# An adaLN block with a long S4D convolution and a ReLU FFN: the last twelve of sixteen kernel values from three powers instead of two more doublings, and wider DVE steps in the shift of h and the butterflies

## The chip, the cores and the metric

The kernel runs on one core of one Trainium2 chip. The metric is the device time of one execution in microseconds, the median over the runs shown. Start times in the trace count from the start of the profiled span.

## The reference

One sequence of 2048 tokens with 576 channels passes through an S4D convolution and then through a ReLU FFN, each behind a layer norm that is shifted and scaled by six vectors made from a condition `c`. What matters of it:

```python
dt = jnp.exp(log_dt)
A = -jnp.exp(log_A_real) + 1j * A_imag          # 576 channels x 128 states
C = (C_real + 1j * C_imag) * dt[:, None]
P = jnp.exp((A * dt[:, None])[:, :, None] * pos[None, None, :])   # pos = 0..2047
K = 2.0 * jnp.einsum("dn,dnl->dl", C, P).real   # the long kernel
y = irfft(rfft(u, 2 * L) * rfft(K, 2 * L))[:L]  # per channel
_A_ref = y + u * D_skip

mod = (_silu(c) @ w_mod).reshape(c.shape[0], 6, 1, -1)
sa, ca, ga, sb, cb, gb = (mod[:, i] for i in range(6))
h = _layernorm(x) * (1 + ca) + sa
x = x + ga * _A_ref(h, ...)
h = _layernorm(x) * (1 + cb) + sb
x = x + gb * (jnp.maximum(h @ w1, 0) @ w2)      # 576 -> 4608 -> 576
```

Everything is float32.

## The kernel before, in words

The tokens are taken in four blocks of 512. The convolution is done blockwise in the frequency domain: `conv(s)` transforms the kernel's block s and the tokens' block s by DFT matmuls on PE (`transform`, PSUM tile `ps_f`, L852), a radix-4 butterfly on DVE (`butterfly1` L864 to 868, `butterfly2` L870 to 881), multiplies spectra of all earlier blocks (`product`, L1032 to 1038), and goes back. The FFN (`ffn`, from L1268) takes 36 chunks of 128 hidden channels for each block, 144 steps in all: PE makes the hidden chunk `hps` (L1332), ACT writes its rounded half `hh` (L1337), DVE the remainder `hl` (L1338), and PE multiplies both by `w2` (L1358).

The program has three parts in time.

*Kernel generation* (`KGen.first`, L318 on). K is needed as a sum over the states of C z^l, where z = exp(A dt). Position l is split as 32 a + b, so a matmul over the 128 states of W1 (sixteen values a, with C in them) and W2 (32 values b) gives the block. This is done in NG = 6 groups of G = 96 channels, each in two half groups u of H = 48. For each group:

- `exps`: PE makes the exponents (tile `ph`), ACT takes Exp of them (tile `E`).
- `turns`: PE makes the phases, ACT rounds them to whole turns (tile `k`, L59), DVE subtracts (L62, `k<-ph,k`). This is done in three pieces; the last holds the powers of z listed in `POWERS`.
- `sines`: ACT takes sines and cosines; DVE and POOL multiply them by the moduli into W2, and `powers` makes Zp, the powers 32, 64, 128 and 256 of z, in PSUM, with the powers 512 and 1024 in `zs` in SBUF. `moduli` multiplies Zp by E on DVE.
- `doubling`: from W1's first value the values two, then four, eight and sixteen. A doubling of m values multiplies the m that are there by the power 32 m, complex: two DVE products (`t` by the real part, `T` by the imaginary part) and two adds. The first two doublings take the whole group; the third (m = 4) and the fourth (m = 8) each half group alone. The adds of the first three are on DVE, those of the fourth on POOL (L68).
- `save`: W1 goes to DRAM for the later blocks; `products`: PE multiplies W2 by W1 (tile `kps`, L71), u = 0 at the end of its own group, u = 1 (`late`) between the phases of the next.

In this part all instructions of PE, ACT, DVE and POOL, but for some copies and memsets on POOL, are kept in the program's order by the recording helpers: `act` L59, `v` L62, `stt` L65, `pool` L68, `matmul` L71. That order is written out by hand in the loop over g: the phases of group g + 1 stand between the doublings of group g.

*Passage to conv(0).* `early` makes h, the normed and shifted tokens of block 0, in stages that the loop calls. In the last group (g = 5) its last stage runs between the third and the fourth doubling: `skip` adds the kernel's skip term to the first kernel tile `kt` (L1263), then h is multiplied by `ca` (L641) and gets `sa` added (L642), one token tile of 576 columns at a time. conv(0) then transforms `kt` (24 outputs with those of h, 48 records on PE), runs the products of the last group, stores its rows to DRAM (`kd`), loads the second tile `kt` back, and goes on to its butterflies and products. The queue of SP carries `kd` and `kt`, that of POOL carries `Rd`.

*The FFN with what remains.* The other blocks' kernels are made by rotating W1 further (`rest`, L482 to 488, products L517), and conv(1) to conv(3) run beneath the FFN. Each is a generator that yields the estimated DVE time of each piece; `step()`, called in each FFN chunk, draws pieces from the generator up to a budget per chunk. The order within the FFN is then made by a scheduler from these pieces. The butterfly's yields are 1.5 for each half of `butterfly1`, then 1.5 and 1.8 in `butterfly2`; those of the products are 1.35 for each instruction.

Of the kernel before, what the change touches and what calls it, by code (L numbers as in the profile page):

```python
# [34 lines left out]
POWERS = (32, 64, 128, 256, 512, 1024)  # L35
# [14 lines left out]
class KGen:  # L50
# [131 lines left out]
    def exps(self, g):  # L182

        E = self.E[g] = []
        for s0, n in ((0, 8), (8, 8), (16, 8), (24, 8), (32, 6)):
            e = self.pt.tile([P, 2, 8 * H], F32, tag="E", bufs=8, name=f"E_{g}")
            e = self.chunk(e, s0, n)
            self.act(e, self.times(g, self.zz[1], s0, n), AF.Exp)
            E.append(e)
            yield  # L190

    def turns(self, g):

        F = self.F[g] = []
        for s0, n in ((0, 8), (17, 8), (32, 6)):
# [66 lines left out]
    def powers(self, g, e, f):  # L262

        Z = self.ps.tile([P, 2, 512], F32, tag="Z", name=f"Zp_{g}")[:, :, 0 : 4 * G]
# [4 lines left out]
        self.act(by_u(Z[:, 1]), f[:, :, 0:4], AF.Sin, scale=-TWO_PI)  # L269
        self.act(by_u(zs[:, :, 1]), f[:, :, 4:6], AF.Sin, scale=-TWO_PI)  # L270
        self.cos(by_u(Z[:, 0]), c[:, :, 0:4])
        self.cos(by_u(zs[:, :, 0]), c[:, :, 4:6])
        for r in (1, 0):
            self.pool(by_u(zs[:, :, r]), by_u(zs[:, :, r]), e[:, :, 4:6], op=ALU.mult)
        self.Z[g] = Z, zs

        def moduli():
            for r in (1, 0):
                self.v(by_u(Z[:, r]), by_u(Z[:, r]), e[:, :, 0:4], ALU.mult)
# [3 lines left out]
    def doubling(self, g, i, u):  # L283

        v, p = self.v, self.pool
        Z = self.Z[g][0]
        m, n = 1 << i, (u.stop - u.start) * H
        W1 = self.W1[g][:, :, u].rearrange("p r u c a -> p r (u c) a")
        X, out = W1[:, :, :, 0:m], W1[:, :, :, m : 2 * m]
        zr, zi = (  # L290
            Z[:, r, i, u.start * H : u.stop * H].unsqueeze(1).unsqueeze(3)
            .broadcast_to([P, 2, n, m])
            for r in range(2)
        )
        if m == 8:
            t = self.pc.tile([P, 16 * H], F32, tag="T0", bufs=2, name="T0")
            T = self.pc.tile([P, 16 * H], F32, tag="T1", bufs=2, name="T1")
        else:
            t = self.pc.tile([P, 8 * H], F32, tag="t", bufs=2, name="t")[:, : 2 * n * m]
            T = self.ps.tile([P, 512], F32, tag="T", name="T")[:, : 2 * n * m]  # L300
        t, T = (x.rearrange("p (r c a) -> p r c a", r=2, c=n) for x in (t, T))
        v(t, X, zr, ALU.mult)
        v(T, X, zi, ALU.mult)
        yield
        add = p if m == 8 else v
        add(out[:, 0], t[:, 0], T[:, 1], op=ALU.subtract)
        add(out[:, 1], t[:, 1], T[:, 0], op=ALU.add)
# [16 lines left out]
    def first(self, setup, mod):  # L324
# [70 lines left out]
        for g in range(NG):  # L395
            self.moduli()
            if g + 1 == NG:
                next(early)
            double = [
                self.doubling(g, i, u)  # L400
                for i, u in (
                    (0, slice(0, 2)), (1, slice(0, 2)), (2, slice(0, 1)), (2, slice(1, 2)),
                    (3, slice(0, 1)), (3, slice(1, 2)),
                )
            ]
# [22 lines left out]
            run(*double[4:])  # L428
# [143 lines left out]
class Body:  # L572
# [34 lines left out]
    def early(self, kg):  # L607
# [32 lines left out]
        for i in (0, 2, 1, 3):  # L640
            kept(nc.vector.tensor_tensor(h[:, i], h[:, i], self.m["ca"], op=ALU.mult))  # L641
            kept(nc.vector.tensor_tensor(h[:, i], h[:, i], self.m["sa"], op=ALU.add))  # L642
# [921 lines left out]
```

## Time and profile before

| | |
|---|---|
| median of three runs | 1333.97 us (1328.8 to 1339.76) |
| profiled execution | 1333.12 us |
| its span | 1331.4 us |
| PE busy | 1209.0 us (91%) |
| DVE busy | 895.4 us (67%) |
| ACT busy | 494.5 us (37%) |
| POOL busy | 162.8 us (12%) |
| mean granted clock of PE | 0.945 |

The busy share of a whole span is a mean over stages with different limits, so it does not say what a saved microsecond is worth. For that the span is cut into windows, and in each the busy time of the engines is compared with the window's length. Rows of a timeline give the start, the length, the engine, the line, the operation with the names of output and inputs, the shape, and after `x` how many neighbouring instructions the row joins; a bracket behind it says how long the engine was idle before it and what ended that. In the chain of waits each row is a piece of the path that ended last. `L62` and its neighbours are helpers, so a row there is told apart by its tiles: `T<-W,Zp` is a product of a doubling, `k<-ph,k` a subtraction of whole turns, `W<-T,T` on POOL the adds of the last doubling.

### The profile page before, as it was taken

The page shows a single profiled execution, that of the slowest core. Times are in us where ns is not written, and L with a number is a line of the kernel's source. Part 1 is how long each engine was busy: PE and PEld are TensorE (multiplying, and loading weights), DVE is VectorE, ACT ScalarE, POOL GpSimd, SP SyncE. Part 2 cuts the span into 40 slices and gives each one's busy share as a digit, 9 for nine tenths or more (in the row PEclk, how much of TensorE's full clock was granted, in tenths as well). Part 3 has the DMA queues.
Part 4 walks back from the last instruction along what each step waited for, and adds up shares of the span by engine and source line. Part 5 has one row for each costly group of instructions (what it writes and reads, how often), then busy time and mean ns, then how long its engine had stood idle before and what let it go on. Part 6 is the DMA issues. An engine that isn't in the chain of part 4 may idle for free.

```text
span 1331.4 us, 25993 instructions
## 1 busy us (share of the span) xinstructions
PE 1209.0 (91%) x10720; PEld 956.7 (72%) x10720; DVE 895.4 (67%) x1324; ACT 494.5 (37%) x863; POOL 162.8 (12%) x260
## 2 busy tenths in 40 slices
PE   4566676989989999999999999999999999999997
PEld 3344554667767687777777887887888888888885
DVE  5989988999986999689468993558995231111112
ACT  5678623222223422622243225433223453232321
POOL 0756502011000100100001000100000000000000
PEclk9557788999999999999999999999999999999999
DMA  8557982989878967799879985868996557666651
GB/s 272 214 221 296 304 307 84 350 296 331 307 253 304 337 224 277 247 402 342 281 276 338 357 321 156 288 203 305 346 363 198 175 181 223 198 198 202 192 168 54
DMA packets 122379, 345.85 MB, mean 260 GB/s; under 512 B 23916, under 2 KB 24212, under 8 KB 111508
## 3 DMA queue, kind: packets, MB, share of 16 engines
q1 hardware_dynamic: 105364, 226.96, 51.2%
q0 software_dynamic: 16384, 115.85, 23.1%
q8 instruction: 84, 1.38, 0.4%
q10 hardware_dynamic: 512, 1.38, 0.3%
q14 instruction: 35, 0.29, 0.1%
HBM read 262.73 MB, written 81.40 MB: 258 GB/s over the span
## 4 chain that ended last, share of the span: by engine, by line
PE 68%; DVE 17%; DMA 7%; issue 4%; ACT 2%; POOL 1%; SPq 0%; ACTq 0%; DVEq 0%; POOLq 0%
PE acc L1358 28%; PE hps L1332 27%; PE ps_f L852 5%; DMA L1d<-w 3%; PE kps L71 2%; PE ph L71 2%; DVE T L482 2%; DVE W1r L484 2%; PE ps_i L1059 2%; PE kps L517 1%; DVE w L1302 1%; DVE W1r L486 1%; DVE W1r L488 1%; DVE w L1314 1%; DVE T L62 1%
## 5 line engine op out<-in xcount | busy, mean ns | idle before, releaser
L1332 PE MATMUL hps<-xh,w 128*128 128x512 f32 x1152 | 395.2, 403 | 1.2 <-ACT xh L47 1.2
L1358 PE MATMUL acc<-w,hh 128*128 128x512 f32 x1152 | 366.4, 400 | 3.3 <-ACT hh L1337 3.2
L1338 DVE SCALAR_TENSOR_TENSOR hl<-hps,hh 128x512 fp32r<-128x512 f32 x144 | 99.0, 687 | 311.5 <-ACT hh L1337 310.8
L1332 PEld LDWEIGHTS hps<-xh,w 128*128 128x128 f32 x1152 | 217.8, 190 | 49.7 <-ACT xh L47 2.5
L1358 PEld LDWEIGHTS acc<-w,hh 128*128 128x128 f32 x1152 | 215.1, 188 | 50.6 <-ACT hh L1337 4.1
L1332 PE MATMUL hps<-xl,w 128*128 128x512 f32 x576 | 228.5, 397 | 0.7 <-DVE xl L47 0.5
L1358 PE MATMUL acc<-w,hl 128*128 128x512 f32 x576 | 223.1, 399 | 1.8 <-DVE hl L1338 1.8
L1337 ACT ACTIVATE hh<-hps 128x512 fp32r<-128x512 f32 x144 | 86.0, 597 | 327.7 <-PE hps L1332 320.5
L1307 ACT ACTIVATE w<-r 128x576 fp32r<-128x576 f32 x141 | 96.7, 686 | 216.5 <-PE acc L1358 216.1
L1332 PEld LDWEIGHTS hps<-xl,w 128*128 128x128 f32 x576 | 109.4, 190 | 24.7 <-DVE xl L47 1.7
L1358 PEld LDWEIGHTS acc<-w,hl 128*128 128x128 f32 x576 | 107.7, 189 | 26.1 <-DVE hl L1338 3.7
L1297 ACT ACTIVATE w<-r 128x640 fp32r<-128x640 f32 x140 | 102.6, 733 | 59.1 <-DMA L1d<-w 53.8
L1332 PE MATMUL hps<-xs,w 128*128 128x512 f32 x288 | 97.8, 409 | 0.0
L71 PE MATMUL kps<-W,W 128*32 128x16 f32 x2304 | 39.6, 210 | 47.3 <-POOL W L68 28.4
L1038 DVE TENSOR_TENSOR Y<-Y,T 128x1152 f32<-128x1152 f32 x60 | 79.3, 1349 | 0.0
L71 PEld LDWEIGHTS kps<-W,W 128*32 128x32 f32 x2304 | 34.8, 143 | 60.7 <-POOL W L68 31.0
L853 ACT ACTIVATE Z<-ps_f 128x288 f32<-128x288 f32 x120 | 49.0, 410 | 70.5 <-PE ps_f L852 68.5
L517 PEld LDWEIGHTS kps<-W1r,W2r 128*32 128x32 f32 x3456 | 45.2, 113 | 38.4 <-issue 19.7
L517 PE MATMUL kps<-W1r,W2r 128*32 128x48 f32 (+2 forms) x3456 | 52.5, 202 | 15.6 <-ACT ker L527 9.4
L1478 POOL DMA_DIRECT2D out_dram<-x x16 | 8.7, 545 | 466.9 <-DVE x L1470 464.5
L1332 PEld LDWEIGHTS hps<-xs,w 128*128 128x128 f32 x288 | 53.2, 188 | 11.1
L1358 PE MATMUL acc<-hh,w 128*128 128x512 f32 x144 | 57.5, 399 | 0.0
(235 smaller groups left out, 1574.5 us busy)
## 6 DMA issues: line engine op xcount, KB each, us to landing
r<-in_w_dram SPq DMA_DIRECT2D x144, 320.0 KB, 6.0
r<-in_w_dram SPq DMA_DIRECT2D x144, 288.0 KB, 3.9
w<-L1d SPq DMA_DIRECT2D x108, 320.0 KB, 4.1
w<-L2d SPq DMA_DIRECT2D x108, 288.0 KB, 2.8
W2r<-W2d POOLq DMA_DIRECT2D x18, 1536.0 KB, 9.4
W2d<-W SPq DMA_DIRECT2D x12, 1536.0 KB, 8.6
Ua<-Ud POOLq DMA_DIRECT2D x15, 1152.0 KB, 9.5
W<-W1d POOLq DMA_DIRECT2D x18, 768.0 KB, 9.6
```

The costliest lines, as they stand in the source:

```text
L71: self.tc.keep_in_program_order(self.nc.tensor.matmul(*args, **kw))
L482: v(T, X, zi, op=ALU.mult)
L517: nc.tensor.matmul(ps[32 * dd : 32 * dd + 32, q, :], W2[:, r, ch], W1[:, r, ch], start=(r == 0), stop=(r == 1),)
L852: nc.tensor.matmul(o, fc[:, n2, c, :], src(n2), start=True, stop=True)
L853: ev = nc.scalar.activation(Z[:, n2, c], ps[:, :PC], AF.Copy)
L1038: v(y, y, T, op=op or ALU.add)
L1297: copy(g - 1)(w1[g][:, 0], r1[g], AF.Copy)
L1307: copy(g)(w[:, 0:D], r2[g], AF.Copy)
L1332: nc.tensor.matmul(ps, a, x, start=(i == 0), stop=(i == 13))
L1337: nc.scalar.activation(hh, ps, AF.Relu)
L1338: nc.vector.scalar_tensor_tensor(hl, ps, 0.0, hh, op0=ALU.max, op1=ALU.subtract)
L1358: nc.tensor.matmul(acc[i], a, x, start=(f == 0 and seen[i] == 1), stop=(f == NF - 1 and seen[i] == (3 if i < 4 else 2)),)
```

## The change

A seventh power, 384, is added to `POWERS`; Zp then holds five powers (32, 64, 128, 256, 384), and the pieces that make powers are 96 columns wider. Only the first two doublings remain. A new generator `quarters` makes the values 4 to 15 of the whole group from the values 0 to 3 and the powers 128, 256 and 384, one broadcast along the other, in four products of 1152 columns on DVE; the two sums are on POOL, in place in W1:

```diff
+    def quarters(self, g):
+
+        v, p = self.v, self.pool
+        W1 = self.W1[g].rearrange("p r u c a -> p r (u c) a")
+        shape = [P, G, 3, 4]
+        X = [W1[:, r, :, 0:4].unsqueeze(2).broadcast_to(shape) for r in range(2)]
+        out = [W1[:, r, :, 4:16].rearrange("p c (j a) -> p c j a", j=3) for r in range(2)]
+        zr, zi = (
+            self.Z[g][0][:, r, 2:NP].rearrange("p j c -> p c j").unsqueeze(3).broadcast_to(shape)
+            for r in range(2)
+        )
+        for r, op in ((0, ALU.subtract), (1, ALU.add)):
+            T = self.pc.tile([P, 12 * G], F32, tag="T0", bufs=2, name="T0")
+            T = T.rearrange("p (c j a) -> p c j a", j=3, a=4)
+            v(out[r], X[r], zr, ALU.mult)
+            if r:
+                yield
+            v(T, X[1 - r], zi, ALU.mult)
+            p(out[r], out[r], T, op=op)
+            yield
```

In the loop over g the first product pair and its sum stand right behind the two doublings, the third product between the first two pieces of `turns`' subtractions, and the fourth with the second sum ahead of the last piece:

```diff
-            run(*double[:2])
+            self.doubling(g, 0)
+            self.doubling(g, 1)
             next(mod, None)
-            run(double[2])
+            next(quarters)
...
-                next(double[3])
+                next(quarters)
                 next(turns)
-                run(late, turns, double[3])
+                run(late, quarters, turns)
             else:
-                run(late, double[3])
+                run(late, quarters)
             if g + 1 == NG:
                 next(early)
             if g > 0:
                 rows(g - 1)
-            run(*double[4:])
```

The shift of h takes two token tiles in an instruction, and the butterflies take two of their four (or eight) pieces at once, with smaller yields:

```diff
-        for i in (0, 2, 1, 3):
-            kept(nc.vector.tensor_tensor(h[:, i], h[:, i], self.m["ca"], op=ALU.mult))
-            kept(nc.vector.tensor_tensor(h[:, i], h[:, i], self.m["sa"], op=ALU.add))
+        for i in range(2):
+            for n, op in (("ca", ALU.mult), ("sa", ALU.add)):
+                m = self.m[n].unsqueeze(1).broadcast_to([P, 2, D])
+                kept(nc.vector.tensor_tensor(h[:, i::2], h[:, i::2], m, op=op))
...
     def butterfly1(self, Z, W):
         v = self.vec.tensor_tensor
-        for i in range(2):
-            v(W[:, 2 * i], Z[:, i], Z[:, i + 2], op=ALU.add)
-            v(W[:, 2 * i + 1], Z[:, i], Z[:, i + 2], op=ALU.subtract)
-            yield 1.5
+        for i, op in enumerate((ALU.add, ALU.subtract)):
+            v(W[:, i::2], Z[:, 0:2], Z[:, 2:4], op=op)
+            yield 1.35
...
-        i, j = (1, 3) if sgn < 0 else (3, 1)
-        v(X[:, i, 0], B[:, 0], Dd[:, 1], op=ALU.add)
-        v(X[:, i, 1], B[:, 1], Dd[:, 0], op=ALU.subtract)
-        v(X[:, j, 0], B[:, 0], Dd[:, 1], op=ALU.subtract)
-        v(X[:, j, 1], B[:, 1], Dd[:, 0], op=ALU.add)
-        yield 1.8
+        X = X.rearrange("p a b c -> p (a b) c")
+        outer, inner = X[:, 2:8:5], X[:, 3:7:3]
+        Br, Dr = B[:, ::-1], Dd[:, ::-1]
+        v(outer, B, Dr, op=ALU.add if sgn < 0 else ALU.subtract)
+        v(inner, Br, Dd, op=ALU.subtract if sgn < 0 else ALU.add)
+        yield 1.5
```

The lines of the changed kernel are one to eight further down: the helper `v` is L63 there, the skip L1271, the shift of h L651, the products of conv(1) L1040 to 1046, `hl` L1346.

The order moves at three places, all on DVE. The first is a group in the middle of the kernel generation (g = 1), from the third doubling to the first tile of the next group's start. `W_1` is the group's W1, `Zp` its powers, `k` the whole turns of group 2. Before, then after:

```order
L62 TENSOR_TENSOR k_866<-ph_867,k_866 128x768
L62 TENSOR_TENSOR t<-W_1_707,Zp_741 128x384
L62 TENSOR_TENSOR T<-W_1_707,Zp_741 128x384
L62 TENSOR_TENSOR k_888<-ph_889,k_888 128x768
L62 TENSOR_TENSOR k_914<-ph_915,k_914 128x2x288
L62 TENSOR_TENSOR W_1_707<-t,T 128x48x4 x2
L62 TENSOR_TENSOR T_923<-W_1_707,Zp_741 128x768
L62 TENSOR_TENSOR T_924<-W_1_707,Zp_741 128x768
L62 TENSOR_TENSOR T_929<-W_1_707,Zp_741 128x768
L62 TENSOR_TENSOR T_930<-W_1_707,Zp_741 128x768
L62 TENSOR_TENSOR Tc<-cc,s_1036 128x192
```
```order
L63 TENSOR_TENSOR W_1_691<-W_1_691,Zp_725 128x96x12
L63 TENSOR_TENSOR T_840<-W_1_691,Zp_725 128x1152
L631 BN_STATS st_844<-x_0_281 128x6 x2
L632 BN_AGGR mv_289<-st_844 128x2
L63 TENSOR_TENSOR k_848<-ph_849,k_848 128x768
L63 TENSOR_TENSOR W_1_691<-W_1_691,Zp_725 128x96x12
L63 TENSOR_TENSOR k_870<-ph_871,k_870 128x768
L63 TENSOR_TENSOR T_891<-W_1_691,Zp_725 128x1152
L63 TENSOR_TENSOR k_894<-ph_895,k_894 128x2x336
L63 TENSOR_TENSOR Tc<-cc,s_1004 128x192
```

The four products that stood behind the last subtraction are gone; the last product now stands ahead of it.

The second place is the last group's passage into the shift of h (`kt` is conv(0)'s first kernel tile, `h` the tokens). Before, then after:

```order
L62 TENSOR_TENSOR t<-W_5_2048,Zp_2082 128x384
L62 TENSOR_TENSOR T<-W_5_2048,Zp_2082 128x384
L62 TENSOR_TENSOR W_5_2048<-t,T 128x48x4 x2
L1263 TENSOR_TENSOR kt_1943<-kt_1943,m_gb 1x4x72
L641 TENSOR_TENSOR h_2099<-h_2099,m_ca 128x576
L642 TENSOR_TENSOR h_2099<-h_2099,m_sa 128x576
```
```order
L63 TENSOR_TENSOR W_5_1968<-W_5_1968,Zp_2002 128x96x12
L63 TENSOR_TENSOR T_2036<-W_5_1968,Zp_2002 128x1152
L63 TENSOR_TENSOR W_5_1968<-W_5_1968,Zp_2002 128x96x12
L63 TENSOR_TENSOR T_2136<-W_5_1968,Zp_2002 128x1152
L1271 TENSOR_TENSOR kt_1863<-kt_1863,m_gb 1x4x72
L651 TENSOR_TENSOR h_2019<-h_2019,m_ca 128x2x576
L651 TENSOR_TENSOR h_2019<-h_2019,m_sa 128x2x576
```

Before, the four products of the fourth doubling stood behind the last operation on h; now all four wide products stand ahead of the skip.

The third place is in the first block of the FFN, between the remainders `hl` no. 30 and 31, where conv(1)'s product runs (`T`, `Y` with spectra `Ka` and `Ua`, `w` and `r` the weights of the FFN). Before, then after:

```order
L1338 SCALAR_TENSOR_TENSOR hl<-hps,hh 128x512
L1313 TENSOR_TENSOR w_6045<-r_5892,w_6045 128x64
L1314 TENSOR_TENSOR w_6045<-r_5892,w_6045 128x512
L1302 TENSOR_TENSOR w_5991<-r_5890,w_5991 128x640
L1036 TENSOR_TENSOR T<-Ka,Ua 128x1152 x2
L1038 TENSOR_TENSOR Y_1_5993<-Y_1_5993,T 128x4x288 x2
L1036 TENSOR_TENSOR T<-Ka,Ua 128x1152
L1338 SCALAR_TENSOR_TENSOR hl<-hps,hh 128x512
```
```order
L1346 SCALAR_TENSOR_TENSOR hl<-hps,hh 128x512
L1044 TENSOR_TENSOR T<-Ka,Ua 128x1152 x2
L1046 TENSOR_TENSOR Y_1_5821<-Y_1_5821,T 128x4x288 x2
L1321 TENSOR_TENSOR w_5911<-r_5759,w_5911 128x64
L1322 TENSOR_TENSOR w_5911<-r_5759,w_5911 128x512
L1310 TENSOR_TENSOR w_5862<-r_5757,w_5862 128x640
L1044 TENSOR_TENSOR T<-Ka,Ua 128x1152 x2
L1046 TENSOR_TENSOR Y_1_5821<-Y_1_5821,T 128x4x288 x2
L1346 SCALAR_TENSOR_TENSOR hl<-hps,hh 128x512
```

Between the two remainders there were five wide operations and are now eight.

More of the change, by code (lines that the diff above doesn't have):

```diff
@@ L194, in turns @@
         F = self.F[g] = []
-        for s0, n in ((0, 8), (17, 8), (32, 6)):
+        for s0, n in ((0, 8), (17, 8), (32, NS - 32)):
             k = self.pt.tile([P, 2, 8 * H], I32, tag="k", bufs=3, name=f"k_{g}")
@@ L398, in first @@
                 next(early)
[L399 to L405, printed above, removed]
+            quarters = self.quarters(g)
             if g + 1 < NG:
```

47 lines of the change are left out of this document (20 added, 27 removed).

## The prediction

> **What bounds the kernel now.** I read the table of windows first, to split the span into stretches with different limits, then the chain of waits for what ends last in each, then the timelines for prices. The windows, as time from the start, length, and busy time of each engine, then granted clock and DMA share:
>
> ```profile
> 35.00:97.00 62.00, 36.03 (x818) 25.30 (x818) 54.92 (x121) 45.35 (x62) 38.55 (x55) 0.50 0.60 224
> 97.00:142.00 45.00, 27.03 (x1063) 21.00 (x1067) 43.29 (x94) 37.47 (x55) 34.40 (x47) 0.69 0.76 282
> 230.00:400.00 170.00, 154.18 (x2602) 119.97 (x2603) 159.35 (x168) 42.58 (x78) 18.52 (x35) 0.96 0.84 305
> 467.00:534.00 67.00, 63.63 (x268) 50.75 (x267) 66.01 (x92) 16.77 (x27) 3.19 (x6) 0.97 0.71 249
> 534.00:1320.00 786.00, 784.46 (x4523) 634.78 (x4522) 416.69 (x579) 277.68 (x491) 39.44 (x69) 1.00 0.75 253
> ```
>
> The columns of engines are PE, PEld, DVE, ACT, POOL. From 534 us on PE is busy 784.46 of 786 us: nothing that DVE saves there can show. Three places are left in which the change can act: the kernel generation up to 142 us, where DVE is busy 54.92 of 62 and 43.29 of 45 us, the passage from it into conv(0), and the stretch 467 to 534 us with the product of conv(1), where DVE is busy 66.01 of 67 us and PE idles 3.4. The rotations of the other blocks (230 to 400 us) run on DVE too, but on lines that the diff does not touch.
>
> The chain of waits through one group and into conv(0) (start, length, engine, what):
>
> ```profile
> 71.59 1.74 DVE T L62 x2
> ...
> 73.40 1.98 POOL W L68 x2
> ...
> 75.42 2.22 PE kps L71 x120
> ...
> 90.64 0.79 PE ph L71 x2
> ...
> 91.52 0.66 ACT k L59
> ...
> 92.20 0.76 DVE k L62
> 92.96 0.53 DVE W L62 x2
> 93.49 3.46 DVE T L62 x4
> ...
> 148.61 13.37 PE ps_f L852 x48
> 161.98 1.75 PE kps L71 x137
> 163.73 6.02 issue
> ...
> 187.18 8.72 DMA Rd<-K
> ```
>
> The loop closes over all engines: PE makes the last phases, ACT rounds them, DVE subtracts, then the doubling to sixteen runs on DVE, two POOL adds finish W1 of the first half group, and PE starts its products. The DVE queue is on the chain, and so is POOL for 1.98 us. After the last group the transforms of conv(0) (ps_f, 13.37 us) follow on PE; they wait for the kt skip (L1263) and the shift of h.
>
> **The change part by part.** Prices first; the fence joins DVE rows and POOL rows (start, length of the row, engine, line, operation, shape):
>
> ```profile
> 109.31 0.55 DVE L62 TENSOR_TENSOR T<-W,Zp 128x384 f32<-128x384 f32 x1
> 109.78 1.61 DVE L62 TENSOR_TENSOR k<-ph,k 128x768 f32<-128x768 f32 x2
> 111.31 0.60 DVE L62 TENSOR_TENSOR W<-t,T 128x192 f32<-128x192 f32 x2
> 111.83 3.54 DVE L62 TENSOR_TENSOR T<-W,Zp 128x768 f32<-128x768 f32 x4
> 115.29 0.35 DVE L62 TENSOR_TENSOR Tc<-cc,s 128x192 f32<-128x192 f32 x1
> ...
> 165.00 2.75 DVE L47 TENSOR_TENSOR W<-Z 128x576 f32<-128x576 f32 x4
> 167.67 2.89 DVE L47 TENSOR_TENSOR U<-W 128x576 f32<-128x576 f32 x6
> ...
> 175.97 2.61 DVE L47 TENSOR_TENSOR Y<-K,U 128x1152 f32<-128x1152 f32 x2
> ```
> ```profile
> 85.57 1.17 POOL L68 TENSOR_TENSOR zs<-zs,E 128x192 f32<-128x192 f32 x2
> 95.29 3.92 POOL L68 TENSOR_TENSOR W<-T,T 128x384 f32<-128x384 f32 x4 [8.27 <-DVE T L62]
> ```
>
> DVE instructions follow each other closer than their lengths say, so I price from start to start. A 384-column product costs 109.78 − 109.31 = 0.47 us, a 768-column one (115.29 − 111.83)/4 = 0.865, so 1.04 ns a column; carried on, 1152 columns cost 1.26. The 1152-column row of conv(0) says 2.61 for two, of which the overlap of about 0.08 comes off: 1.27. I take 1.27. The two small adds cost 111.83 − 111.31 = 0.52.
>
> *DVE in a group.* Gone are the doubling from four to eight, twice (0.47 + 0.47 + 0.52) = 2.9, and the four products of the last doubling, 3.46: together 6.4. New are four products, 5.1. The moduli grow by 2 × 96 columns (0.2 us) and the last subtraction by 96 (0.1). Each group is 1.0 us of DVE lighter.
>
> *What of it reaches the end of a group.* Between ACT's last rounding and the first product on PE stood subtraction 0.76, adds 0.53, two products 1.74 and two POOL adds 1.98. Now the last DVE product stands ahead of the third subtraction, behind the second. A POOL add of 384 columns costs 0.98 and one of 192 half of 1.17, 0.585: 2.06 ns a column, so 0.98 + 768 × 2.06 ns = 2.6 for 1152 (by plain proportion 2.9, from above). In the group that ends at 97.3 us ACT's second rounding, a row of 0.81 us at 90.09 (below), frees the second subtraction; DVE has the product into out[1] in front of it until about 91.5, then 0.86 + 1.27 + 2.6 and PE starts at 96.3, where now it starts after the adds of 95.29, at 95.29 + 1.98 = 97.3: −1.0.
>
> ```profile
> 90.09 0.81 ACT L59 ACTIVATE k<-ph 128x768 int32<-128x768 f32 x1 [0.72 <-PE ph L71]
> 91.52 0.65 ACT L59 ACTIVATE k<-ph 128x576 int32<-128x576 f32 x1 [0.62 <-PE ph L71]
> 79.70:91.40 11.70, 11.70 (x250) 8.18 (x250) 8.25 (x21) 6.02 (x8) 7.33 (x13) 0.50 0.70 282
> ```
>
> That holds for the two groups in which PE paces the loop (the window 79.70 to 91.40 has PE busy all 11.70 us at clock 0.50): −2.0. In the three later ones ACT is the busy one beside DVE (37.47 of 45), and ACT gets wider work: (0.81 − 0.65)/192 = 0.83 ns a column, 96 columns more in about five operations, 0.4 us a group, +1.2. I carry −0.8 into the last group; the bounds are −4.9 (all DVE time saved passes through) and +2.0 (nothing saved, ACT's 0.4 in all five). POOL's 1.3 us more a group lie in its idle time (38.55 busy of 62); without that cover they would cost as much.
>
> The Trainium skill ("TensorE: Matmul & The Clock Gate", "Part 1: The HAM clock gate (the "warmup" mystery)") says that the clock rises after some 3.4 us of sustained activity; by it any gap closed in the loop would speed PE up. The window of 11.70 busy us at 0.50 does not agree, so the sum keeps 0.50.
>
> *The passage to conv(0).* Rows of DVE, and a pair of DVE and POOL:
>
> ```profile
> 144.77 0.55 DVE L62 TENSOR_TENSOR t<-W,Zp 128x384 f32<-128x384 f32 x1
> ...
> 147.96 0.44 DVE L1263 TENSOR_TENSOR kt<-kt,m_gb 1x288 f32<-1x288 f32 x1
> 148.33 0.74 DVE L641 TENSOR_TENSOR h<-h,m_ca 128x576 f32<-128x576 f32 x1
> ...
> 157.61 4.65 DVE L47 TENSOR_TENSOR W<-Z 128x576 f32<-128x576 f32 x4
> ```
> ```profile
> 156.05 4.92 POOL L68 TENSOR_TENSOR W<-T,T 128x384 f32<-128x384 f32 x4 [8.37 <-DVE T L62]
> ```
>
> In the last group only the doubling to eight (147.96 − 144.77 = 3.2) stood ahead of the kt skip; the doubling to sixteen came behind the shift of h. Now all four wide products, 5.1, stand ahead: +1.9. The second POOL add then runs beside the shift of h. The rows show what that does: four butterfly adds, which read two SBUF operands, took 4.65 beside POOL's adds and 2.75 alone, and POOL's four took 4.92, where 3.92 is usual. They take turns. So the first pair of h operations (2.6) can end up to 2.6 late, 5.2 after the skip; PE needs h after the 16 records of mm_K, 13.37/48 × 16 = 4.5 after it: +0.8. The skill ("SBUF — State Buffer", "Who interferes with whom") calls this an exclusive lock in which the second to issue waits for the whole instruction; the rows agree, and it speaks against the change, since one wait is now 2.6 and not 0.98. The wider shift (four operations of 1152 for eight of 576) is worth under a microsecond and ends behind mm_K's cover: nothing.
>
> *Butterflies.* One takes 2.67 + 2.81 = 5.48 now (from 165.00 to 167.67, then 2.89 less the overlap of 0.08). In 1152-column steps and two of 576: 2 × 1.27 + 2 × 0.66 + 2 × 0.67 = 5.2, so 0.28 each. In conv(0) the chain waits 8.72 us for a DMA from 187.18 on, and what comes ahead of that is covered by it; one and a half butterflies behind it count: −0.4. From 534 us on PE covers them.
>
> *conv(1).* The butterflies' yields are smaller (5.7 against 6.3 in all), so the generator reaches the products earlier: the order of DVE shows 25 wide operations between the hidden tiles no. 25 and 31, where there were 21, with two butterflies in both.
>
> ```profile
> 467.08 0.69 DVE L1338 SCALAR_TENSOR_TENSOR hl<-hps,hh 128x512 fp32r<-128x512 f32 x1 [1.14 <-ACT hh L1337]
> 519.78 0.68 DVE L1338 SCALAR_TENSOR_TENSOR hl<-hps,hh 128x512 fp32r<-128x512 f32 x1
> 522.56 1.07 PE L1358 MATMUL acc<-w,hl 128*128 128x512 f32 x4
> 500.42 10.30 DMA Ua<-Ud
> ```
>
> These are hl no. 25 and 31 and PE's use of the latter. Four wide operations more, 4 × 1.27, less two cheaper butterflies, 0.56, put hl 31 back by 4.5. PE took it 2.2 after it was there (522.56 − 519.78 − 0.6), so PE loses 4.5 − 2.2 = 2.3. The bounds are −1.7 (DVE bound, six cheaper butterflies pass in full) and +4.5 (no slack); the load of Ua, 10.30 long, is on the chain already and could be met earlier, within that bound.
>
> *Sum.* The profiled execution is 1333.1, 1.7 over its span of 1331.4; the runs' median is 1334.0 (1328.8 to 1339.8), so a run may lie 0.4% off by itself. Group carry −0.8, passage +1.9 and +0.8, butterflies of conv(0) −0.4, conv(1) +2.3: +3.8, and 1333.1 + 3.8 = 1336.9, say **1337**, own range 1332 to 1342.
>
> **The rivals.**
>
> *B, the savings pass.* Five groups at −1.0, passage +1.9, conv(0) −0.4, conv(1) −1.7: −5.2, 1328. For it: DVE busy 43.29 of 45. Against: ACT and PE pace the loop beside it. Should PE's clock step up a group earlier, 11.70 us at 0.69 for 0.50 take 8.5, −3.2 a group; three groups give 1318.
>
> *C, slower: the operand price.* The new products read W1 in runs of four of every sixteen and powers across three strides. One row has a strided reading dearer:
>
> ```profile
> L62 DVE TENSOR_TENSOR t<-W,Zp 128x192 f32<-128x192 f32 x6 | 2.9, 477 | 0.2
> ```
>
> The 192-column product on W1's single values takes 477 ns, where Tc of the same size took 0.35: 0.12 us per 192, 0.73 per 1152-column product, 2.9 a group. Against 1.0 saved: five groups +9.6, passage 1.9 + 0.8 + 2.9, −0.4, +2.3: +17, 1350. It decides from 0.25 us extra, so from 1.52 us a product. Against it: the 384-column product reads runs of four already and costs 0.47.
>
> *D, the second POOL add wins the race.* The kt skip reads two SBUF operands; if the add comes first, the skip waits 2.6 us and all of conv(0) with it: 1340. For it: the turn-taking at 157.61. Against: the skip stands right behind the product, with no semaphore to travel.
>
> *E, it does not reach the end.* PE's gap of 6.02 us behind the transforms absorbs the passage, and hl 31 keeps its slack: 1333.
>
> **How the numbers follow.** Forecast 0.40, E 0.22, B 0.20, C 0.10, D 0.08. About 1% of the time, 13 us, is what a measurement of this kernel can tell from no change: only C (1350) passes it upwards, 0.10, and a quarter of B with the clock's step downwards, 0.05; the rest, 0.85, is no change. The range leaves out C and B's lower part and gives B and D a run's spread of some 0.3 to 0.5%: 1325 to 1347.
>
> **What would show it.** T and W of L63 at 1.27 us apart; over 1.5 means C. POOL adds of 2.6 us. PE's first product of the second group's W1 one microsecond earlier than 97.3. The kt skip some 1 to 2 us later than 147.96 and directly behind a wide product; a gap of 2.6 there means D. In conv(1), PE idle in the 67 us stretch of about 5.7 instead of 3.4; idle at 3.4 or less says that the move of the products cost nothing. The forecast is wrong if the profiled span moves by more than 9 us either way.

## The result, and the profile after

The changed kernel takes 1345.8 us (median of six runs, 1341.7 to 1350.9); the kernel before, beside it, 1331.9 us (six runs, 1328.7 to 1339.8). The ratio is 1.0088 with a 95% interval of 1.0063 to 1.0114: 0.9% or 12 us slower (the two medians lie 13.9 us apart), where 1337 with a range of 1325 to 1347 was forecast. By its ratio the size lies within what the forecast called no change (1%), but the interval leaves out 1: it is a loss, three times the 4 us that the prediction worked out. Two runs of before that were taken beside the experiments, of 2392 and 2384 us, are slow ones and stand in no ratio.

The profiled execution of the changed kernel took 1343.3 us, its span is 1341.5 us, before 1331.4: 10.1 us to account for. DVE has less to do and the kernel is slower; these are the first lines of its page:

```profile
span 1341.5 us, 25833 instructions
...
PE 1216.2 (91%) x10720; PEld 959.8 (72%) x10720; DVE 883.1 (66%) x1180; ACT 498.3 (37%) x863; POOL 172.2 (13%) x248
```

ACT's eviction of each hidden chunk (`hh`, one for each of the 144 FFN steps) is a good clock for comparing two traces. Its rows no. 0, 25, 37, 72 and 143, first of before, then of after (start, length, engine, line, operation):

```profile
230.47 0.60 ACT L1337 ACTIVATE hh<-hps 128x512 fp32r<-128x512 f32 x1 [2.36 <-PE hps L1332]
466.45 0.60 ACT L1337 ACTIVATE hh<-hps 128x512 fp32r<-128x512 f32 x1 [0.58 <-PE hps L1332]
560.64 0.60 ACT L1337 ACTIVATE hh<-hps 128x512 fp32r<-128x512 f32 x1 [1.04 <-PE hps L1332]
833.26 0.60 ACT L1337 ACTIVATE hh<-hps 128x512 fp32r<-128x512 f32 x1 [2.49 <-PE hps L1332]
1314.29 0.60 ACT L1337 ACTIVATE hh<-hps 128x512 fp32r<-128x512 f32 x1 [5.75 <-PE hps L1332]
```
```profile
231.06 0.60 ACT L1345 ACTIVATE hh<-hps 128x512 fp32r<-128x512 f32 x1 [2.37 <-PE hps L1340]
466.70 0.60 ACT L1345 ACTIVATE hh<-hps 128x512 fp32r<-128x512 f32 x1 [0.57 <-PE hps L1340]
568.05 0.60 ACT L1345 ACTIVATE hh<-hps 128x512 fp32r<-128x512 f32 x1 [2.92 <-PE hps L1340]
842.85 0.60 ACT L1345 ACTIVATE hh<-hps 128x512 fp32r<-128x512 f32 x1 [2.49 <-PE hps L1340]
1323.80 0.60 ACT L1345 ACTIVATE hh<-hps 128x512 fp32r<-128x512 f32 x1 [5.75 <-PE hps L1340]
```

The difference is +0.6 at no. 0, +0.2 at no. 25, +7.4 at no. 37, +9.6 at no. 72 and +9.5 at the end. So in this pair of profiles nearly nothing of what happened in the first 465 us, where most of the diff acts, is left in the end; 7.2 us are lost between no. 25 and 37, where conv(1) ends beneath the first block of the FFN, and another 2.0 between no. 67 and 72, where conv(2) ends (10.9 and 12.5 late at no. 70 and 68, of which part is caught up). Three windows of after that answer to those shown of before:

```profile
97.00:142.00 45.00, 28.83 (x957) 21.71 (x950) 38.37 (x70) 37.27 (x52) 34.86 (x39) 0.60 0.76 282
...
467.00:534.00 67.00, 58.71 (x236) 45.31 (x235) 64.62 (x75) 15.15 (x24) 3.18 (x6) 0.95 0.65 237
534.00:1320.00 786.00, 782.63 (x4514) 632.99 (x4513) 416.08 (x536) 279.06 (x492) 39.34 (x69) 1.00 0.76 255
```

In the kernel generation DVE's saved time has become idle time (38.37 busy of 45, before 43.29). In the stretch from 467 us PE's idle time grew from 3.4 to 8.3 us while DVE stays nearly full. The PE rows of after with a wait in that stretch (the bracket: idle before, and what ended it) show five kinds of wait, of which before had one of 2.77 for `hh` and two of 0.2 and 0.3 for `hl`:

```profile
480.61 0.50 PE L1366 MATMUL acc<-w,hl 128*128 128x512 f32 x1 [0.84 <-DVE hl L1346]
489.92 1.21 PE L1067 MATMUL ps_i<-V,gc 128*128 128x288 f32 x4 [1.08 <-DVE V L881]
498.75 1.24 PE L1067 MATMUL ps_i<-V,gc 128*128 128x288 f32 x4 [1.19 <-DVE x L1072]
500.68 1.20 PE L1366 MATMUL acc<-w,hl 128*128 128x512 f32 x4 [0.69 <-DVE hl L1346]
519.53 1.20 PE L1366 MATMUL acc<-w,hh 128*128 128x512 f32 x4 [2.47 <-ACT hh L1345]
522.63 0.80 PE L1366 MATMUL acc<-hh,w 128*128 128x512 f32 x1 [1.89 <-DVE w L1321]
```

While PE stands idle at one of these rows, it starts none of the FFN's other matmuls either. What made DVE late is, first of all, a wait that before did not have. The DVE timeline of after, ahead of conv(1)'s first product (`T<-K,Ua`), and later, ahead of the second half's:

```profile
451.73 0.69 DVE L1322 TENSOR_TENSOR w<-r,w 128x512 fp32r<-128x512 f32 x1
458.02 1.36 DVE L1044 TENSOR_TENSOR T<-K,Ua 128x1152 f32<-128x1152 f32 x1 [5.61 <-DMA Ua<-Ud]
459.30 2.62 DVE L875 TENSOR_TENSOR W<-Z 128x1152 f32<-128x1152 f32 x2
...
514.48 0.69 DVE L1346 SCALAR_TENSOR_TENSOR hl<-hps,hh 128x512 fp32r<-128x512 f32 x1
517.27 2.63 DVE L1044 TENSOR_TENSOR T<-Ka,Ua 128x1152 f32<-128x1152 f32 x2 [2.11 <-issue]
```

DVE has run through its work by 452.42 and waits 5.61 us for the load of Ua. In the kernel before, two narrow butterfly steps and three pieces of the FFN's weights stand ahead of that product; DVE comes to it at 453.50, the load has landed at 453.48, and it starts without a wait. So DVE is 1.1 us earlier, and the load lands 4.5 us later, at 458.00: it goes out 2.6 later (448.65 for 446.06) and takes 9.4 us for 7.4. Why it goes out later can be seen some 20 us ahead, in rows of DVE and POOL, first of before, then of after:

```profile
430.72 0.74 DVE L866 TENSOR_TENSOR W<-Z 128x576 f32<-128x576 f32 x1
435.48 0.76 DVE L866 TENSOR_TENSOR W<-Z 128x576 f32<-128x576 f32 x1
440.01 0.55 POOL L843 DMA_DIRECT2D Rd<-K  x1 [3.54 <-DVE K L880]
446.06 0.54 POOL L839 DMA_DIRECT2D Ua<-Ud  x1 [2.85 <-DMA Rd<-K]
```
```profile
435.76 2.63 DVE L875 TENSOR_TENSOR W<-Z 128x1152 f32<-128x1152 f32 x2 [0.73 <-ACT Z L862]
441.36 0.55 POOL L852 DMA_DIRECT2D Rd<-K  x1 [4.61 <-DVE K L888]
448.65 0.53 POOL L848 DMA_DIRECT2D Ua<-Ud  x1 [3.96 <-DMA Rd<-K]
```

A narrow step of the butterfly of K reads two of the four parts of Z, so before, half of the first stage is done from 430.72 on, while ACT still writes the other parts. A wide step reads all four, and both wide steps wait for ACT's last write. K is finished later, its store (`Rd<-K`) goes out 1.35 later and takes 6.7 us for 5.5, and POOL issues the load of Ua only when that store has landed. The same holds for the second butterfly of U, which stands behind the waiting product in after: ACT's last write to its Z ends at 455.94 (455.53 + 0.41), so the wide steps could not have filled the first 3.5 us of the wait; of before's narrow steps half had run by 452.1. From there on DVE is behind in a stretch where it has no time to spare.

### The profile page after: what moved, and what is told of

Its sections match the earlier page's. It is cut to its first block, busy times and chain, and to the rows that moved or that the text cites. A ratio compares the mean times of both kernels' runs of the same rounds, so it can differ in the third digit from the quotient of the medians.

```text
span 1341.5 us, 25833 instructions
## 1 busy us (share of the span) xinstructions
PE 1216.2 (91%) x10720; PEld 959.8 (72%) x10720; DVE 883.1 (66%) x1180; ACT 498.3 (37%) x863; POOL 172.2 (13%) x248
## 4 chain that ended last, share of the span: by engine, by line
PE 66%; DVE 14%; DMA 8%; issue 6%; ACT 3%; POOL 1%; SPq 0%; POOLq 0%; ACTq 0%; DVEq 0%
PE acc L1366 27%; PE hps L1340 27%; PE ps_f L861 4%; PE kps L525 3%; DMA Ua<-Ud 3%; DMA L1d<-w 2%; PE ps_i L1067 2%; PE kps L72 2%; DVE T L1044 1%; PE ph L72 1%; DVE Y L1046 1%; DVE W L875 1%; ACT c L60 1%; DVE T L490 1%; POOL W L69 1%
## 5 line engine op out<-in xcount | busy, mean ns | idle before, releaser
L1346 DVE SCALAR_TENSOR_TENSOR hl<-hps,hh 128x512 fp32r<-128x512 f32 x144 | 99.3, 690 | 317.9 <-ACT hh L1345 317.3
```

What stands on the lines that cost most here:

```text
L1346: nc.vector.scalar_tensor_tensor(hl, ps, 0.0, hh, op0=ALU.max, op1=ALU.subtract)
```

## The experiments

All ratios are to the kernel before, with 95% intervals; e1 to e12 were timed 5 to 12 times each, beside 25 to 34 runs of before on one chip. Beside them stands what the profile of each form lost between hh no. 25 and 37 (conv(1)) and between 67 and 72 (conv(2)), against before. Single runs of one kernel scatter by some 0.5% either way, and between profiles the first 465 us alone differ by −5.4 to +4.1 us, so these two columns tell the forms apart better than their total times. They come from one profile of each form; the four forms with the old butterflies in conv(1) to conv(3) and e9, whose conv(1) is the old one, show how far the first column scatters by itself, −0.7 to +0.6.

| form | conv(1) to (3): instructions, yields | ratio | hh 25 to 37 | hh 67 to 72 |
|---|---|---|---|---|
| changed kernel | wide, new | 1.0088 [1.0063, 1.0114] | +7.2 | +2.0 |
| e1 | narrow, old | 0.9991 [0.9969, 1.0012] | −0.2 | 0.0 |
| e2 | wide, new (nothing else changed) | 1.0062 [1.0032, 1.0091] | +7.4 | +1.9 |
| e3 | wide, old | 1.0043 [1.0020, 1.0066] | +1.9 | +1.0 |
| e4 | narrow, new (nothing else changed) | 1.0006 [0.9983, 1.0030] | +5.2 | +0.2 |
| e5 | wide, new; loads first | 1.0061 [1.0035, 1.0088] | +6.1 | +0.2 |
| e6 | wide, new; smaller budget | 1.0128 [1.0083, 1.0173] | +19.1 | +0.5 |
| e7 | narrow, old; kt skip first | 1.0031 [1.0007, 1.0054] | +0.6 | 0.0 |
| e8 | narrow, old; loads first | 1.0014 [0.9990, 1.0037] | −0.7 | 0.0 |
| e9 | conv(1) narrow, old; others wide, new | 1.0038 [1.0015, 1.0062] | +0.1 | +2.1 |
| e10 | narrow, old (conv(0) wide) | 1.0032 [1.0012, 1.0053] | +0.1 | 0.0 |
| e11 | conv(1) wide, old; others narrow, old | 1.0032 [1.0008, 1.0056] | +3.6 | 0.0 |
| e12 | conv(1) narrow, new; others narrow, old | 1.0060 [1.0038, 1.0081] | +4.1 | 0.0 |

Three theories stood at first. M: the smaller yields let the meter of the FFN (the budget that `step()` keeps) put more convolution work ahead of what PE waits for. W: the wide instructions themselves do it. G: the kernel generation with its quarters leaves something late that shows only here.

### e1 and e2: which half of the change

e1 takes the butterflies back, e2 makes only them.

```diff
 e1: the changed kernel, with
-        for i, op in enumerate((ALU.add, ALU.subtract)):
-            v(W[:, i::2], Z[:, 0:2], Z[:, 2:4], op=op)
-            yield 1.35
+        for i in range(2):
+            v(W[:, 2 * i], Z[:, i], Z[:, i + 2], op=ALU.add)
+            v(W[:, 2 * i + 1], Z[:, i], Z[:, i + 2], op=ALU.subtract)
+            yield 1.5
...
 e2: the kernel before, with the opposite edit
```

> The changed kernel with the butterflies of before (narrow steps, yields 1.5, 1.5, 1.5, 1.8); the quarters in kernel generation and the wide shift of h stay. Theory M (the smaller yields let conv(1) put more products ahead of the remainders hl 29 to 33): the loss of 9 us between the chunks 27 and 37 of the FFN goes, about 1333 us, ratio to before 1.000 to 1.002. Theory W (the wide steps hold DVE longer at a time): the same, about 1333. Theory G (the loss comes out of kernel generation, by what it leaves late): still about 1344.

Measured: 1333.8 us, ratio 0.9991, and nothing lost at either place.

> The kernel before with only the new butterflies and their smaller yields; kernel generation and the shift of h as before. M: all the loss is here, about 1344 us, ratio about 1.008, with hh no. 37 some 7 us later than before. W: also about 1344. G: about 1332, a little faster than before.

Measured: 1340.6 us, ratio 1.0062, 7.4 and 1.9 us lost at the same two places as in the changed kernel. G falls: the loss is in the butterflies of conv(1) and conv(2), whatever the kernel generation does.

### e3 and e4: instructions or yields

```diff
 e3: the changed kernel, with
-            yield 1.35
+            yield 1.5
...
         v(inner, Br, Dd, op=ALU.subtract if sgn < 0 else ALU.add)
-        yield 1.5
+        yield 1.8
...
 e4: the kernel before, with
-            yield 1.5
+            yield 1.35
...
-        yield 1.8
+        yield 1.5
```

> The whole change, but the butterflies yield 1.5, 1.5, 1.5 and 1.8 as before; the wide instructions stay. Between the remainders 25 and 31 the order has 22 wide products, as before 21 and in the changed kernel 25. M: about 1333 us, no slower than before. W: about 1344, the loss stays, since the wide instructions do. G: about 1344.

> The kernel before with nothing changed but the yields of the butterflies, 1.35, 1.35, 1.5, 1.5; every instruction is that of before, only the order within the FFN moves (24 wide products between the remainders 25 and 31). M: about 1344 us, ratio about 1.008. W: about 1332. G: about 1332.

Measured: e3 1339.7, e4 1336.3 us. Neither theory alone is borne out: e3 should have lost nothing by M, and loses 1.9 and 1.0 at the two places; e4 should have lost nothing by W and loses 5.2 in conv(1). (e3 and e4 each lose some 3 us more between no. 37 and 53, with PE waiting 2.6 and 2.9 for ACT's `ker` in the rotations, which no edit touches.) The total times say the opposite of the columns, e3 slower than e4, but their intervals overlap and cannot decide. So the two causes were tried apart in conv(1) alone.

### e9, e10, e11 and e12: conv(1) by itself

All four are the changed kernel with a choice of butterfly for each convolution; conv(0), whose order is written out by hand, keeps the wide one. The cut is that of e11 and e12; e9 and e10 choose in the same way between two forms.

```diff
-    def butterfly(self, Z, X, sgn):
+    def butterfly(self, Z, X, sgn, narrow=0):
         W = self.spec("W")
-        yield from self.butterfly1(Z, W)
-        yield from self.butterfly2(W, X, sgn)
+        yield from (self.butterfly1, self.third1, self.narrow1, self.narrow1)[narrow](Z, W)
+        yield from (self.butterfly2, self.third2, self.narrow2, self.narrow2)[narrow](W, X, sgn)
...
-            yield from self.butterfly(Z, U, -1)
+            yield from self.butterfly(Z, U, -1, s)
```

`narrow` holds the form of before; `third` is the wide form with the old yields in e11 and the narrow form with the new yields in e12. In e9 conv(1) alone is `narrow`, in e10 conv(1) to conv(3) are.

> The whole change, but conv(1) alone keeps the narrow butterflies with their yields of before; conv(0), conv(2) and conv(3) have the new ones. If the loss sits in conv(1), the 7 us between hh 25 and hh 37 are gone and the 2 us at hh 67 to 71 (conv(2), where PE waits for V and x) stay: about 1335 to 1337. If conv(2) and conv(3) carry it, still about 1343.

> Quarters, wide shift of h and the wide butterflies of conv(0), where the order is written out by hand; conv(1) to conv(3) have the narrow butterflies with the yields of before. Both theories: nothing is lost in the FFN, hh 25 to 37 as before within 0.3 us, and conv(0) gains up to 0.4: 1331 to 1334, the fastest form of the change.

> e10, but conv(1) has the wide instructions with the yields of before, so the order from hl 28 on is that of before. Theory M (yields make the order, the order makes the loss): hh 37 against hh 25 within 1 us of before, time as e10. Theory W (the wide instructions themselves): 5 us or more. The profile of e3 had 1.9 there.

> e10, but conv(1) has the narrow instructions of before with the new yields 1.35, 1.35, 1.5, 1.5, so only the order of conv(1) moves (eight wide products between hl 30 and 31 instead of five). M: hh 37 against hh 25 is 5 us later than before and the time 5 us over e10. W: the same as e10.

Measured: e9 1336.2, e10 1336.2, e11 1337.4, e12 1341.0 us. In e9 conv(1)'s loss is gone and conv(2)'s 2.1 us are all there, as expected of the place. In e10 nothing is lost in either, as expected, but its total is 0.3% over before and not the fastest of the forms. e11 loses 3.6 in conv(1), e12 4.1: each cause by itself loses time, and 3.6 + 4.1 = 7.7 (or, from the first pair, 1.9 + 5.2 = 7.1) is close to the 7.2 of both together. M and W are each about half right in these profiles. The total times show it less well: e12 is 4.7 us over e10, but e11 only 1.2, which their scatter hides; e3 against e1, 5.9, is the clearer pair for the wide instructions.

How the wide instructions lose shows in the DVE timeline of e11 at the place shown of the changed kernel:

```profile
452.75 1.36 DVE L1083 TENSOR_TENSOR T<-K,Ua 128x1152 f32<-128x1152 f32 x1 [5.63 <-DMA Ua<-Ud]
454.03 2.62 DVE L914 TENSOR_TENSOR W<-Z 128x1152 f32<-128x1152 f32 x2
```

The same wait of 5.6 us as in the changed kernel. All six forms with wide instructions in conv(1) have it (e2 5.3, e3 4.4, e5 5.8, e6 4.0, e11 5.6, the changed kernel 5.6), and none of those with narrow ones comes near (before 0, e1 0.4, e7 1.6, e8 0.3, e9 0.9, e10 1.4, e12 0.7, e4 2.3). POOL's wait for K ahead of its store tells them apart as well: 4.61 in all six, 3.54 or 3.55 in the other eight. So the wide steps make K and with it the load late, and bring the product early. No run let the load go out sooner and kept the wide steps, so how much of the 3.6 is this wait is argued and not shown.

How the yields lose shows in e12, which has not that wait. Its DVE meets the load of the second half instead, and PE waits behind:

```profile
517.86 2.63 DVE L1084 TENSOR_TENSOR T<-Ka,Ua 128x1152 f32<-128x1152 f32 x2 [2.37 <-issue]
```
```profile
500.98 1.21 PE L1406 MATMUL acc<-w,hl 128*128 128x512 f32 x4 [0.69 <-DVE hl L1386]
520.02 1.20 PE L1406 MATMUL acc<-w,hh 128*128 128x512 f32 x4 [2.63 <-ACT hh L1385]
523.21 0.79 PE L1406 MATMUL acc<-hh,w 128*128 128x512 f32 x1 [1.99 <-DVE w L1361]
```

Its DVE order has eight wide operations between `hl` 30 and 31, in before five, and the weight half `w` (L1361) stands among them; PE waits 1.99 for it. The profile names nothing that ended the 2.37, but the load of Ua landed 0.08 us before the product started. With the new yields and everything else as it was DVE comes to this product 10.9 us after its load went out, with the old ones 12.4, and the load takes some 13: a wait of 2.1 to 2.6 in the changed kernel, e2, e4 and e12, and of 0.4 to 0.9 in before, e1, e3, e7, e9, e10 and e11.

### e5 and e8: the loads ahead of the store

Theory D was that the queue of POOL sets the stretch: the load of Ua for the second half's product waits behind the store of K.

```diff
-            if s and s + 1 < NB:
+            if s and s + 1 < NB and p == 0:
                 self.save(self.Kd[s][p], K)
...
                     nxt = pair(order[i + 1])
+                    if i == 0 and p == 1 and s + 1 < NB:
+                        self.save(self.Kd[s][p], Ks[p])
```

> The whole change, but in conv(1) and conv(2) the store of the second half's combined spectrum (Kd) is issued behind the loads for the product instead of ahead of them, so that the last load of Ua need not wait on POOL's queue for DVE's K. Theory D (in conv(1) the chain DVE K, store Kd, load Ua of 10.3 us, product sets the end of the stretch): Ua starts near 499.7 instead of 504.24, the 2.1 us for which DVE idles ahead of the product are gone, the loss falls by 3 to 5 us, to about 1340. Theory M (only the number of wide operations ahead of hl and of the weight halves counts; it stays at 25): about 1344.

> e1 (old butterflies, quarters, wide shift of h) with the loads of the product ahead of the store of Kd as in e5. D: Ua starts about 4 us earlier, DVE's idle of 0.6 ahead of the product goes and PE's wait for hh of 2.5 with it, 1 to 3 us faster than e1. M: the same as e1.

Measured: e5 1340.0 us, the time that D gave (though the interval of its ratio overlaps the changed kernel's), but not for D's reason as far as its profile shows. Ua went out at 497.01, and DVE's wait ahead of that product fell from 2.11 to 0.38, yet conv(1) still lost 6.1, because PE now waits 3.4 for `hl` behind the products that start earlier:

```profile
516.46 1.25 PE L1368 MATMUL acc<-w,hl 128*128 128x512 f32 x4 [3.40 <-DVE hl L1348]
```

What it gained was conv(2)'s loss (2.0 to 0.2). On the old butterflies (e8, 1333.6 us, 1.0014) the loads gain nothing that shows. D's wait by itself is not what conv(1) loses: where it goes away in e5, a PE wait for `hl` takes its place. The wait of 5.8 ahead of the first half's product remains in e5.

### e6: a smaller budget

If the meter lets too much through, a budget cut in the proportion of the yields (5.7 to 6.3) should mend it.

```diff
-            room = (7.5, 7.0, 7.0, 7.0)[g // NF] - sum(recent[-3:])
+            room = (6.8, 6.35, 6.35, 6.35)[g // NF] - sum(recent[-3:])
...
-            while done[0] < target and v < min(room, 2.7) and pe < 2:
+            while done[0] < target and v < min(room, 2.45) and pe < 2:
```

> The whole change with the small yields, but the budget for each FFN chunk is cut in the same proportion: room 6.8 and 6.35 instead of 7.5 and 7.0, at most 2.45 instead of 2.7 a chunk. The order then has 16 wide products between the remainders 25 and 31, before 21, changed kernel 25. M: the loss goes, 1332 to 1336, PE idle between 465 and 590 us about 3.6 instead of 8.3. D: the load stays where it stands behind K, but the product comes later, so it also gains, 1336 to 1340. If neither holds, 1344.

Measured: 1350.8 us, ratio 1.0128: a clear miss. Up to hh no. 25 its profile was 5.4 us ahead of before and then lost 19.1. Its waits are not those of the others (PE for the transposes of conv(1)'s result):

```profile
PE ps_t L1162 <- ACT h L1154: 5.3, 3, 4.1
PE acc L1366 <- DVE hl L1346: 2.2, 2, 2.0
```

(Engine, line, what it waits for; us in total, times, longest.) conv(1) makes the input of the FFN's second block, so it must be done by hh no. 36. The waits fit a budget that pushes conv(1) against that end, where a larger share ahead of `hl` makes PE wait earlier; budgets between the two were not tried.

### e7: does the passage count

```diff
             else:
-                run(late, quarters)
+                run(late)
             if g + 1 == NG:
                 next(early)
+                run(quarters)
```

> The kernel with the quarters, the wide shift of h and the old butterflies (e1), but in the last group the second pair of wide products and their sum stand behind the shift of h, so the kt skip is not behind them. The kt skip comes 2.5 us earlier than in e1. Theory A (what the passage loses is taken up by PE's gaps behind the transforms and the loads): the same as e1 within 1 us, and the first hh is within 0.5 us of e1's. Theory P (the passage is on the path that ends last): 2 to 3 us faster than e1.

Measured: the kt skip came at 148.88, in e1 at 151.69, 2.8 us earlier, and the first matmul of the FFN at 225.37, in e1 at 224.35: not earlier. The time, 1336.6 us, is no better than e1's 1333.8. P falls. A is missed too, to the other side: it allowed 0.5 us at the first hidden chunk and 1 us in the time, and e7 is 1.0 and 2.8 later there. Why stays open; the intervals of the two ratios overlap.

## Why the prediction was right and wrong

**The forecast as a whole.** The direction came true, and 1345.8 lies in the wide range, 1.2 us below its upper end. But it lies above the forecast's own range (1332 to 1342), and the span moved by 10.1 us, more than the 9 that the prediction had named as the sign that the forecast is wrong. The upper end was there for rival D with a run's spread; D did not happen. That the number fell inside is luck; one term of the sum, conv(1), was a third of what it measured.

**What bounds the kernel.** The three places were the right ones. From 534 us on, "nothing that DVE saves there can show" was not contradicted by any run, but the reverse does not follow: a DVE that is later by its order still stopped PE for 2 us at hh no. 67 to 72, with DVE busy two thirds of the time there (46.0 of 70 us from 780 to 850).

**The prices** came out, one after another. In group 1 of after:

```profile
83.91 1.35 DVE L63 TENSOR_TENSOR W<-W,Zp 128x1152 f32<-128x1152 f32 x1
85.17 1.35 DVE L63 TENSOR_TENSOR T<-W,Zp 128x1152 f32<-128x1152 f32 x1
```
```profile
93.18 2.65 POOL L69 TENSOR_TENSOR W<-W,T 128x1152 f32<-128x1152 f32 x1 [3.94 <-DVE T L63]
```

A wide product costs 85.17 − 83.91 = 1.26 (forecast 1.27), a POOL sum 2.65 (2.6), and a butterfly, from 486.48 to 491.69, 5.2 (5.2). That rules out rival C, which needed 1.52.

**The groups.** PE's products of the second group's W1 start at 95.89 instead of 97.32: −1.4, forecast −1.0. But the later groups give it back: the same start moves from 115.74 to 116.03 and from 135.30 to 136.22, and the first product that follows the two whole-group doublings of the last group from 144.77 to 146.67. The carry was +1.9, not −0.8. DVE waits there for ACT (6.6 us in the window 97 to 142, before 0.9; its busy time there fell by 4.9), and ACT's rounding of the last piece got wider (0.73 us for 0.65); that this is the whole cause is argued and was not tried.

**The passage.** Rows of after:

```profile
146.67 1.35 DVE L63 TENSOR_TENSOR W<-W,Zp 128x1152 f32<-128x1152 f32 x1
...
151.73 0.56 DVE L1271 TENSOR_TENSOR kt<-kt,m_gb 1x288 f32<-1x288 f32 x1
152.22 1.34 DVE L651 TENSOR_TENSOR h<-h,m_ca 128x1152 f32<-128x1152 f32 x1
153.59 3.69 DVE L651 TENSOR_TENSOR h<-h,m_sa 128x1152 f32<-128x1152 f32 x1
```
```profile
149.37 6.70 POOL L69 TENSOR_TENSOR W<-W,T 128x1152 f32<-128x1152 f32 x2 [2.71 <-DVE T L63]
```
```profile
152.50 6.21 PE L861 MATMUL ps_f<-kt,fcK 128*128 128x288 f32 x16 [1.57 <-issue]
158.55 7.92 PE L861 MATMUL ps_f<-h,fcU 128*128 128x288 f32 x32
...
171.92 1.94 PE L72 MATMUL kps<-W,W 128*32 128x16 f32 x128 [3.69 <-issue]
175.92 1.31 PE L72 MATMUL kps<-W,W 128*32 128x16 f32 x80 [2.06 <-issue]
```

The skip stands 5.1 behind the first wide product (3.2 before): +1.9, as forecast. The turns between DVE and POOL came too: an h operation of 1.34 took 3.69 beside the second sum, and two sums of 2.65 took 6.70. The skip itself, which stands ahead of the sum, was not held (rival D falls). The transforms of h start 4.5 us later, those of kt 3.9: +0.6, forecast +0.8. The Trainium skill ("SBUF — State Buffer", "Who interferes with whom") has the lock as one that the first to issue holds for its whole instruction; the 2.35 us that the h operation lost, nearly one sum of 2.65, agree. And then all of it vanished: PE's two gaps behind the transforms shrank from 6.02 and 3.70 to 3.69 and 2.06, and of 4.5 us 0.6 were left at the first hidden chunk, where generation, passage and conv(0) were put at +1.5 together. For this part rival E was right, and in e7 a skip 2.8 us earlier gained nothing. That generation, passage and conv(0) together came out 0.9 from the forecast is chance: the carry was 2.7 off, and the gaps that swallowed it were put at nothing.

What the generation and the passage cost in the total time stays open within some microseconds. The four forms that lose nothing in conv(1) and conv(2) (e1, e7, e8, e10) have ratios of 0.9991 to 1.0032, 1.0017 in the mean, about 2 us; none of them is clearly faster than the kernel before.

**conv(1): the step that failed.** The prediction named the place, the sign and one of two mechanisms (smaller yields, "so the generator reaches the products earlier", `hl` 31 late), but its term of +2.3 measured +7.2, with 2.0 in conv(2) that it had put at nothing. PE's idle time in the stretch from 467 us was 8.3, forecast 5.7. It "put hl 31 back by 4.5", from counted operations; it came 9.1 later (528.90, before 519.78). The two rows of after, no. 25 and 31:

```profile
470.19 0.68 DVE L1346 SCALAR_TENSOR_TENSOR hl<-hps,hh 128x512 fp32r<-128x512 f32 x1
528.90 0.69 DVE L1346 SCALAR_TENSOR_TENSOR hl<-hps,hh 128x512 fp32r<-128x512 f32 x1
```

By rows: `hl` 25 was 3.1 late already (470.19, before 467.08), behind the wait for Ua of 5.61; the four wide operations less the cheaper butterflies give the 4.5; and the wait at 517.27 is 1.5 longer than before (2.11 for 0.64): 9.1 together. The count of operations was right, and the waits were what was left out. Of the two loads of Ua the prediction had seen the second half's (500.42, "on the chain already") and kept what meeting it earlier could cost within its bound of +4.5; the first half's, whose wait is the larger, it did not name. That a wide step waits for the last part of its input, and so makes K, its store and that load late, it left out altogether: it priced the wide butterfly as 0.28 cheaper, and e11 lost 3.6 with it. Put into the prediction's own sum, 9.1 gives 9.1 − 2.2 = 6.9, close to the 7.2; but PE has no wait at `hl` 31 in the trace of after, it had lost its time ahead of that.

A second thing was left out. `hl` is not all that PE needs from DVE: the weight half `w` (1.89), V (1.08) and x (1.19) each stopped PE once, and these 4.2 us are most of the 4.7 by which PE's idle time grew between 465 and 590 us (116.71 busy of 125, before 121.38). Part of the rest is PE's clock. Windows of after, then one of before:

```profile
515.00:521.90 6.90, 3.26 (x14) 2.04 (x12) 4.79 (x5) 3.02 (x5) 0.00 (x0) 1.00 0.57 224
522.00:528.70 6.70, 6.07 (x14) 4.65 (x15) 6.70 (x8) 0.00 (x0) 0.00 (x0) 0.50 0.55 186
528.80:535.00 6.20, 6.07 (x25) 4.38 (x25) 6.20 (x10) 1.84 (x3) 0.00 (x0) 1.00 0.18 44
```
```profile
516.90:520.20 3.30, 3.30 (x9) 2.58 (x8) 3.30 (x4) 1.31 (x2) 0.00 (x0) 0.50 0.39 150
```

From 522 on, within the second of the waits of 2.47 and 1.89, the granted clock is 0.50 for 6.7 us; in before, behind the one wait of 2.77, for 3.3. These 3.4 us more at half the clock cost, as an estimate, 1.7: the added idle time cost about a third more than its length (1.7 on 4.7). Some 0.8 of the 7.2 stays unexplained. Rival B (the savings pass) found no support: the four forms without a loss in the FFN are about 2 us over before in the mean.

## What to carry to other kernels

Where a scheduler orders the work from estimates, a faster instruction and its smaller estimate are two changes, and either can cost more than the instruction saves: here 0.28 us a butterfly was bought for 9 us of PE. Before changing either in a stretch where the helper engine is full, list every tile that the bound engine takes from it (not only the one that is late now) and every DMA wait in the helper's queue, and ask what stands behind each when it is reached sooner. Ask of each wider step, too, which of its inputs comes last: a narrow one may start on the first. And where order is written by hand and gaps follow, as in the passage here, a few microseconds of delay may cost nothing: look for the next gap before adding the term to the sum.

## What was not expected of the hardware

In the generation PE was busy for 11.70 of 11.70 us at a granted clock of 0.50 (the prediction's window of before), while in the FFN two waits of 2.5 and 1.9 us within a few microseconds are followed by 6.7 us at 0.50, and the one wait of 2.8 of before by 3.3. The total time of one kernel scatters by 1.0 to 1.3% between runs on one chip (25 runs of the kernel before, 1325.6 to 1339.0 us; 30 others, 1323.8 to 1340.4), and the profiles, one for each form, suggest where: up to hh no. 25 they differ by −5.4 to +4.1 us from before, and behind it the forms with old butterflies stay within 1.5 of it. What varies there stays open.
